# Moving the on-chip buffers of a matmul-bound attention + softplus-MLP kernel to other addresses

## The chip, the cores and the metric

The kernel runs on one core of a Trainium2 chip. The core has a matrix engine (TensorE, "PE" in the profile; its weight loads are listed apart as "PEld"), a vector engine (VectorE, DVE), a scalar engine (ScalarE, ACT), GpSimd (POOL), the SyncE queue that issues nearly all transfers here (SP), 16 DMA engines, a state buffer of 128 partitions (SBUF) and a matmul accumulator (PSUM). The metric is device microseconds of one execution; lower is better.

## The reference

Attention without a softmax, normalised per row, followed by an MLP with a softplus:

```
kv  = einsum('bhsd,bhse->bhde', k, v)          # B=8, H=8, S=576, D=64
o   = einsum('bhsd,bhde->bhse', q, kv)
x   = o / sqrt(mean(o*o, -1) + 1e-6) * g_norm  # then (B,H,S,D) -> (4608, 512)
h   = x @ w_in                                 # 512 -> 2048
g   = max(h, 0) + log1p(exp(-|h|))             # softplus
out = g @ w_out                                # 2048 -> 512
```

q, k and v come as float32, the weights as float64, of which the kernel reads the two 32-bit words.

## The kernel before, in words

Both factors of the large products are split into two or three float32r pieces, so that TensorE's products of pieces add up to the wanted precision. A buffer of pieces is therefore three times as long as its matrix. Every product on TensorE takes two operands from SBUF: the weights (`lhsT`, 128 x 128, loaded by a LDWEIGHTS) and the streamed operand (`rhs`, 256, 384 or 512 columns of 4 bytes in each partition). The weights of product i+1 are loaded while product i streams; in the trace such a load starts 2 to 5 ns after the start of product i in the dense stretches.

The work has two stages. In the first (`step`, L830; 64 steps up to about 360 us) blocks of 384 tokens go through weight chunks held in SBUF. `mm1` (L844) streams `units` with the weights `pieces`: twelve products of 384 columns. Softplus and the split of its result into `gv` follow on ACT and DVE, and `mm2` (L851) streams `pieces` (w_out) with the weights `gv`: three times three products of 512 columns. In between lie the attention (L677, L701, L719, L757), the conversion of the weights, and in the first 60 us warm-up products of the identity matrix (L1210) where TensorE would be idle.

In the second stage (`wide_step`, L1024; 48 steps, two passes over 9 groups of 512 tokens) the first product is formed from seven sub-products of half blocks: `product` (L1039, L1046) streams 256 columns of `units`, `early` or `turned` with weights from `pieces`, `w12` to `w14` or `half0` to `half2`. `mm2` (L1111, L1116) streams `pieces` (or a `w`) with weights from `gv0`/`gv1` (`gvt`) and `g0`/`g1` (`gt`). In both stages DVE and ACT make the pieces (L855, L859, L1095, L1103, L1106, L1109 for the results; L1006, L1009, L1012 for the inputs).

The order of all instructions on all engines is laid down by a planner (`Plan.order`, L90) from due times and assumed durations, before anything runs. It knows rings of slots and no addresses. Buffers come from two pools, `const` and `sb`. `space` (L286) makes a named buffer the first time it is asked for, and `new` (L314) hands it, or a part of it, to a slot; what `new` doesn't find by name it takes from `sb` under the slot's own tag, among them the small `r_0` and `r_1` of the row norms (`rows`, L688; L705 to L713). The allocator places buffers one after the other in the order in which they are first asked for, so that order decides the addresses.

The built program puts them, in bytes within a partition, here (the last number is the address modulo 512):

```
units    17312  416     raw      160672 416     half0  198560 416
pieces   54176  416     g1       164768 416     half1  201632 416
loads   127904  416     m_0..m_7 168864 416 ..  w14    204736 448
gv1     136096  416     w12      184224 416     half2  210912 480
early   144288  416     w13      192416 416     gv0    213984 480
g0      156576  416     ident_r   16512 128     turned 222176 480
```

All parts of buffers that TensorE takes begin at multiples of 512 bytes within them. So a streamed operand and the weights loaded meanwhile lie 0 bytes apart modulo 512 in 3,475 of the 4,581 float32r products, 32 or 64 bytes apart in 1,082, and otherwise in the rest (mostly beside `ident_r`). Apart from `ident_r` and `w14`, the operands begin at 32 modulo 64.

Of the kernel before, what the change touches and what calls it, by code (L numbers as in the profile page):

```python
# [8 lines left out]
F32 = mybir.dt.float32  # L9
F32R = mybir.dt.float32r  # L10
# [8 lines left out]
P = 128  # L19
# [7 lines left out]
def shaped(x, shape, dtype):  # L27

    n = 1
    for d in shape[1:]:  # L30
        n *= d
    words = n // 2 if dtype == BF16 else n
    x = x[:, :words]
    if x.dtype != dtype:
        x = x.bitcast(dtype)
    names = "abcdef"[:len(shape) - 1]
    if len(names) < 2:
        return x
    return x.rearrange(f"r ({' '.join(names)}) -> r {' '.join(names)}", **dict(zip(names, shape[1:])))
# [162 lines left out]
def kernel(  # L202
# [25 lines left out]
    B, H, S, D = q.shape  # L228
# [13 lines left out]
    WIDE = 512  # L242
# [25 lines left out]
    const = ctx.enter_context(tc.tile_pool(name="const", bufs=1))  # L268
    sb = ctx.enter_context(tc.tile_pool(name="sb", bufs=1))
# [8 lines left out]
    half = const.tile([P, H], F32, name="half")  # L278
    big = const.tile([P, 1], F32, name="big")
    over = const.tile([P, 2 * KF], F32, name="over")  # L280
    scale = const.tile([P, 1], F32, name="scale")

    PIECE = 3 * d_model
    spaces = {}

    def space(name, words, late, dtype=F32):  # L286

        if (name, late) not in spaces:
            spaces[name, late] = sb.tile([P, words], dtype, tag=name, name=f"{name}_{int(late)}")
        return spaces[name, late]  # L290

    units = sb.tile([P, 6, PIECE], F32R, name="units")
    pieces = sb.tile([P, 12, PIECE], F32R, name="pieces")
    loads = sb.tile([P, 4 * d_model], F32, name="loads")

    minus_r = space("gv1", 4 * WIDE, False, F32R)[:, 3 * NT:3 * NT + P]
    early = space("early", 2 * PIECE, False)
    kvs = [shaped(early[:, 2 * PIECE - (i + 1) * NP * D:2 * PIECE - i * NP * D], [P, NP, D], F32) for i in range(2)]
    tails = [shaped(space("g0", 2 * WIDE, False)[:, i * H * D:], [P, H, D], F32) for i in range(2)]
# [14 lines left out]
    def new(s, shape, dtype=F32):  # L314
        r, i = s.ring, s.place
        bank = {"h": i, "s0": 4, "s1": 5, "s2": 6, "tp": 7, "s3": 7}.get(r)
        if r == "o":
            s.tile = banks[:, 2:4].rearrange("r b (a k t) -> r (b a) k t", k=2, t=P)[:, :, i]
        elif r == "ab":
            s.tile = banks[:, 2 * i:2 * i + 2]  # L320
        elif bank is not None:
            s.tile = shaped(banks[:, bank], shape, dtype)
        elif r == "xv":
            s.tile = shaped(units[:, 3 * i:3 * i + 3].rearrange("r a b -> r (a b)"), shape, dtype)
        elif r == "qa":
            s.tile = shaped(early, shape, dtype)
        elif r in ("xb", "u1"):
            s.tile = shaped(space("turned", PIECE, r == "u1", F32R if r == "u1" else F32), shape, dtype)
        elif r == "u":
            s.tile = shaped(units[:, 2 * i:2 * i + 2].rearrange("r a b -> r (a b)") if i < 3 else  # L330
                            space("early", 2 * PIECE, True, F32R), shape, dtype)
        elif r == "w":
            s.tile = shaped(pieces[:, i] if i < 12 else space(f"w{i}", PIECE, True, F32R), shape, dtype)
        elif r == "n":
            s.tile = shaped(space(f"w{12 + i // 3}", PIECE, False)[:, i % 3 * d_model:], shape, dtype)
        elif r == "wh":
            s.tile = shaped(space(f"half{i}", PIECE // 2, True, F32R), shape, dtype)
        elif r == "gvp":
            s.tile = shaped(space(f"gv{i}", 4 * WIDE, True, F32R), shape, dtype)
        elif r == "gv":  # L340
            s.tile = shaped(space(f"gv{i}", 4 * WIDE, False, F32R), shape, dtype)
        elif r == "g":
            s.tile = shaped(space("half2", PIECE // 2, False)[:, i * NT:], shape, dtype)
        elif r == "x":
            s.tile = shaped(space(f"half{i}", PIECE // 2, False), shape, dtype)
        elif r == "rawb":
            s.tile = shaped(space("g1", 2 * WIDE, False), shape, dtype)
        elif r in ("e", "xl"):
            s.tile = shaped(loads[:, i * (d_model if r == "e" else 2 * d_model):], shape, dtype)
        else:  # L350
            s.tile = sb.tile(shape, dtype, tag=f"{r}_{i}", name=f"{r}_{i}")
        return s.tile
# [42 lines left out]
    def weight(j, pos, fetch_pos, behind):  # L395
# [5 lines left out]
        def fetch():  # L401
            src = w_source(j)
            x = new(raw, [P, d_model, words], U32 if wide else F32)
            nc.sync.dma_start(
                out=x.rearrange("p n w -> p (n w)").rearrange("p (a f) -> p a f", a=src.shape[1]), in_=src)

        f = add("SP", 450, fetch, (), fetch_pos, [raw], size=1800, behind=behind)
        if wide:
# [5 lines left out]
            def square():  # L414
                nc.scalar.activation(new(sq, [P, d_model], BF16), raw.tile.bitcast(BF16)[:, :, 3],
                                     func=AF.Square, scale=2.0 ** 47)

            def high1():
                nc.vector.tensor_scalar(out=new(t, [P, d_model], U32), in0=words_of()[1], scalar1=3,
                                        scalar2=0x3FFFFFF8, op0=ALU.logical_shift_left, op1=ALU.bitwise_and)  # L420
# [825 lines left out]
```

## Time and profile before

| | |
|---|---|
| median of 3 runs | 875.08 us (872.5 to 876.75) |
| the profiled execution: span from first to last instruction | 869.7 us |
| TensorE busy, share of the span | 853.5 us, 98% |
| VectorE busy | 704.4 us, 81% |
| ScalarE busy | 521.9 us, 60% |
| moved by DMA | 167 MB, 192 GB/s |

The profiled execution is known by its span alone; it ends 5.4 us below the median and 2.8 us below the fastest run, which is what lies before its first and after its last instruction, and the spread of the runs.

TensorE's products overlap in the profile: the "mean ns of one" is a product's time from its start to its modelled end, while the next one starts earlier. What a product costs is the distance from its start to the start of the next one, called its pitch here. The chain of work shows it: so many products in so many microseconds.

### The profile page before, as it was taken

The page shows a single profiled execution, that of the slowest core. Times are in us where ns is not written, and L with a number is a line of the kernel's source. Part 1 is how long each engine was busy: PE and PEld are TensorE (multiplying, and loading weights), DVE is VectorE, ACT ScalarE, POOL GpSimd, SP SyncE. Part 2 cuts the span into 40 slices and gives each one's busy share as a digit, 9 for nine tenths or more (in the row PEclk, how much of TensorE's full clock was granted, in tenths as well). Part 3 has the DMA queues.
Part 4 walks back from the last instruction along what each step waited for, and adds up shares of the span by engine and source line. Part 5 has one row for each costly group of instructions (what it writes and reads, how often), then busy time and mean ns, then how long its engine had stood idle before and what let it go on. Part 6 is the DMA issues. An engine that isn't in the chain of part 4 may idle for free.

```text
span 869.7 us, 17041 instructions
## 1 busy us (share of the span) xinstructions
PE 853.5 (98%) x6464; PEld 758.2 (87%) x6464; DVE 704.4 (81%) x995; ACT 521.9 (60%) x980; POOL 75.9 (9%) x79
## 2 busy tenths in 40 slices
PE   7799999999999999999999999999999999999998
PEld 5578888888888999988999988898999899999996
DVE  7888889888788888898888798878788766788873
ACT  5766665436344467766667655654867555566654
POOL 0351223111113300000000000000000000000000
PEclk9999999999999999999999999999999999999999
DMA  9999998989894755436655546545364752777864
GB/s 267 281 243 209 265 239 262 178 243 216 216 183 120 186 168 176 146 99 216 202 155 163 171 148 205 189 150 170 121 196 139 230 165 96 237 239 240 242 188 127
DMA packets 239778, 167.07 MB, mean 192 GB/s; under 512 B 106320, under 2 KB 198736, under 8 KB 239696
## 3 DMA queue, kind: packets, MB, share of 16 engines
q1 hardware_dynamic: 239392, 165.86, 68.4%
q8 instruction: 50, 0.82, 0.4%
q14 instruction: 32, 0.26, 0.1%
q10 hardware_dynamic: 304, 0.13, 0.1%
HBM read 112.98 MB, written 52.95 MB: 191 GB/s over the span
## 4 chain that ended last, share of the span: by engine, by line
PE 94%; DMA 3%; DVE 2%; ACT 1%; issue 0%; POOL 0%; SPq 0%; DVEq 0%; ACTq 0%
PE banks L1116 31%; PE banks L1046 28%; PE banks L851 16%; PE banks L844 15%; PE banks L701 2%; PE banks L677 2%; DMA early<-in_q_dram 1%; DMA loads<-in_v_dram 1%; DMA g<-in_v_dram 1%; DMA raw<-in_moe_w_in_dram 0%; PE banks L719 0%; PE banks L1210 0%; DVE units L624 0%; DVE half L713 0%; DVE units L627 0%
## 5 line engine op out<-in xcount | busy, mean ns | idle before, releaser
L1116 PE MATMUL banks<-pieces,gv 128*128 128x512 f32 x768 | 240.2, 394 | 0.0
L1116 PE MATMUL banks<-pieces,g_False 128*128 128x512 f32 x384 | 150.2, 391 | 0.0
L1116 PEld LDWEIGHTS banks<-pieces,gv 128*128 128x128 f32 x768 | 133.1, 189 | 19.1
L851 PE MATMUL banks<-pieces,gv 128*128 128x512 f32 x576 | 145.8, 397 | 0.0
L844 PE MATMUL banks<-units,pieces 128*128 128x384 f32 x768 | 145.3, 337 | 0.0
L844 PEld LDWEIGHTS banks<-units,pieces 128*128 128x128 f32 x768 | 135.3, 188 | 5.0
L851 PEld LDWEIGHTS banks<-pieces,gv 128*128 128x128 f32 x576 | 106.1, 188 | 21.1
L1046 PEld LDWEIGHTS banks<-units,pieces 128*128 128x128 f32 x840 | 112.7, 190 | 7.0 <-ACT banks L1091 0.4
L1046 PE MATMUL banks<-units,pieces 128*128 128x256 f32 x840 | 116.9, 282 | 0.0
L866 ACT ACTIVATE half<-banks 128x384 f32<-128x384 f32 x64 | 31.4, 491 | 95.2 <-PE banks L844 93.9
L1106 DVE TENSOR_TENSOR gv<-g_True,gv 128x1024 fp32r<-128x1024 f32 x47 | 57.5, 1223 | 37.4 <-ACT gv L1103 37.4
L1116 PEld LDWEIGHTS banks<-pieces,g_False 128*128 128x128 f32 x384 | 72.1, 188 | 16.1
L1046 PEld LDWEIGHTS banks<-units,w 128*128 128x128 f32 x504 | 67.6, 189 | 4.1 <-ACT banks L1091 0.2
L1046 PE MATMUL banks<-units,w 128*128 128x256 f32 x504 | 70.5, 282 | 0.0
L709 POOL TENSOR_TENSOR r<-r,half 128x8 f32<-128x8 f32 x36 | 62.3, 1730 | 3.0
L1109 DVE SCALAR_TENSOR_TENSOR g_False<-gv 128x1024 fp32r<-128x1024 f32 x47 | 57.6, 1225 | 1.5
L1095 DVE TENSOR_TENSOR g_True<-banks,g_True 128x512 f32<-128x512 f32 x48 | 33.1, 690 | 30.7 <-PE banks L1046 24.6
L1009 DVE TENSOR_TENSOR units<-loads,units 128x1024 fp32r<-128x1024 f32 x42 | 51.2, 1219 | 6.4 <-ACT units L1006 6.3
L1073 ACT ACTIVATE g_True<-banks 128x256 f32<-128x256 f32 x96 | 36.8, 384 | 32.6 <-PE banks L1046 31.9
L911 ACT ACTIVATE m<-banks 128x512 f32<-128x512 f32 x72 | 42.1, 595 | 19.7 <-PE banks L1116 13.8
L1012 DVE SCALAR_TENSOR_TENSOR units<-units 128x1024 fp32r<-128x1024 f32 x42 | 51.4, 1224 | 1.8
L1006 ACT ACTIVATE units<-loads 128x1024 fp32r<-128x1024 f32 x42 | 44.4, 1058 | 12.5 <-PE banks L1046 12.5
(115 smaller groups left out, 1248.1 us busy)
## 6 DMA issues: line engine op xcount, KB each, us to landing
loads<-x SPq DMA_DIRECT2D x180, 128.0 KB, 2.6
part<-m SPq DMA_DIRECT2D x72, 256.0 KB, 3.0
m<-part SPq DMA_DIRECT2D x72, 256.0 KB, 3.4
loads<-form SPq DMA_DIRECT2D x45, 256.0 KB, 3.3
form<-loads SPq DMA_DIRECT2D x36, 256.0 KB, 2.9
raw<-in_moe_w_in_dram SPq DMA_DIRECT2D x16, 512.0 KB, 4.6
loads<-in_k_dram SPq DMA_DIRECT2D x32, 256.0 KB, 4.6
loads<-in_v_dram SPq DMA_DIRECT2D x32, 256.0 KB, 4.6
```

What stands on the lines that cost most here:

```text
L709: nc.gpsimd.tensor_tensor(out=r.tile, in0=r.tile, in1=half, op=ALU.pow)
L844: nc.tensor.matmul(hp, lhsT=w_in.tile[:, i, kd * P:(kd + 1) * P], rhs=xv.tile[:, i, kd], start=(m == 0), stop=(m == 3 * KD - 1))
L851: nc.tensor.matmul(mine[i].tile, lhsT=gv.tile[:, m, i * P:(i + 1) * P], rhs=w_out.tile[:, m], start=(c == cs[0] and m == 0), stop=(c == cs ...
L911: a = add("ACT", 690 if ph == LAST else 600, lambda: nc.scalar.activation(new(ot, [P, d_model]), bank.tile, func=AF.Copy, scale=scale if p ...
L1006: nc.scalar.activation(part_of(0, F32R), xl.tile if m > 1 else xl.tile[:, 0], func=AF.Copy, scale=DOWN)
L1009: nc.vector.tensor_tensor(out=part_of(1, F32R), in0=xl.tile if m > 1 else xl.tile[:, 0], in1=part_of(0), op=ALU.subtract)
L1012: nc.vector.scalar_tensor_tensor(out=part_of(2, F32R), in0=part_of(1), scalar=-RADIX, in1=part_of(0), op0=ALU.mult, op1=ALU.add)
L1046: nc.tensor.matmul(place(q), lhsT=w[:, m, at:at + P], rhs=dst.tile[:, m, v, kd] if u < 6 else dst.tile[:, m, kd], start=(u == 0 and not m ...
L1073: nc.scalar.activation(dst, src, func=AF.Softplus, scale=1.0 + E)
L1106: nc.vector.tensor_tensor(out=gvt(1, F32R), in0=gt(), in1=gvt(0), op=ALU.subtract)
L1109: nc.vector.scalar_tensor_tensor(out=gt(F32R), in0=gvt(1), scalar=-RADIX, in1=gvt(0), op0=ALU.mult, op1=ALU.add)
L1116: nc.tensor.matmul(mine[i].tile, lhsT=(gvt(m, F32R) if m < 2 else gt(F32R))[:, c, i * P:(i + 1) * P], rhs=outs[c].tile[:, m], start=fresh ...
```

## The change

Only addresses change. A small constant tile `roots` takes the place of the two `r` buffers, and `gap0` fills up to a multiple of 64 bytes. All buffers with streamed `units`, `early`, `turned` and all weights of `mm2` (`gv`, `g`) are asked for first and begin at 0 modulo 512; 256 bytes of `gap1` follow, and then the buffers of weight pieces, whose addresses are 256 modulo 512, and everything that is only for ACT, DVE and DMA.

```diff
+    roots = const.tile([P, 2, H], F32, name="roots")
+    const.tile([P, 8], F32, name="gap0")
 
     PIECE = 3 * d_model
+    SHIFT = 64
...
     units = sb.tile([P, 6, PIECE], F32R, name="units")
+    for i in (0, 1):
+        space(f"gv{i}", 4 * WIDE, False, F32R)
+        space(f"g{i}", 2 * WIDE, False)
+    space("early", 2 * PIECE, False)
+    space("turned", PIECE, False)
+    sb.tile([P, SHIFT], F32, name="gap1")
     pieces = sb.tile([P, 12, PIECE], F32R, name="pieces")
+    for i in range(3):
+        space(f"w{12 + i}", PIECE, False)
+        space(f"half{i}", PIECE // 2, False)
     loads = sb.tile([P, 4 * d_model], F32, name="loads")
...
+        elif r == "r":
+            s.tile = roots[:, i]
```

The instructions of every engine, their order and their waits are the same in the two built programs, one by one; only the addresses and names of buffers differ. Afterwards the distance modulo 512 is 256 in 4,078 of the 4,581 float32r products, 0 in 479 (where `mm1` or `product` hands over to `mm2` or back, and among the warm-ups) and 128 in the rest, and every operand begins at a multiple of 64.

## The prediction

> **What bounds the kernel now.** I read the page's shares first, then the chain that ended last, then the stages, then single stretches of TensorE.
>
> ```profile
> span 869.7 us, 17041 instructions
> PE 853.5 (98%) x6464; PEld 758.2 (87%) x6464; DVE 704.4 (81%) x995; ACT 521.9 (60%) x980; POOL 75.9 (9%) x79
> PEclk9999999999999999999999999999999999999999
> PE 94%; DMA 3%; DVE 2%; ACT 1%; issue 0%; POOL 0%; SPq 0%; DVEq 0%; ACTq 0%
> ```
>
> TensorE is the bound: 94% of the chain is its own products, at full granted clock, so waits are a small matter. What counts is the pitch, the time from one product's start to the next one's. The chain in order of time gives it, as stretches of one line:
>
> ```profile
> 0.72 3.74 DMA raw<-in_moe_w_in_dram
> 6.61 5.81 DMA g<-in_v_dram
> 12.90 6.89 DMA early<-in_q_dram
> 19.81 6.71 DMA loads<-in_v_dram
> ...
> 129.71 4.18 PE banks L851 x18
> 138.36 4.17 PE banks L844 x24
> ...
> 444.24 2.85 PE banks L1046 x24
> 454.76 2.86 PE banks L1046 x24
> 457.63 2.78 PE banks L1116 x12
> ```
>
> Per product: 256 columns 2.86/24 = 119.2 ns (L1046), 384 columns 4.17/24 = 173.8 ns (L844), 512 columns 4.18/18 = 232.2 ns (L851) and 2.78/12 = 231.7 ns (L1116). What would be the pitch without a loss? In the first 3 us, before TensorE speeds up, warm-up products of 512 columns start 426 to 427 ns apart in the trace; at exactly double that rate they would be 213.3 ns apart, 0.4167 ns a column, so 106.7, 160.0 and 213.3 ns for the three widths. Against this each product now loses 12.5, 13.8, 18.9 and 18.4 ns. Products by line: 2016 (L1046), 768 (L844), 576 (L851), 1152 (L1116). Together 25.2 + 10.6 + 10.9 + 21.2 = 67.9 us. That is the most there is to win on TensorE.
>
> Next, what stands behind TensorE in the stages (columns: PE, PEld, DVE, ACT, POOL busy):
>
> ```profile
> 60.00:130.00 70.00, 69.44 (x714) 60.35 (x713) 61.39 (x106) 42.67 (x85) 16.94 (x17) 1.00 0.99 241
> 130.00:360.00 230.00, 230.00 (x1943) 205.70 (x1942) 194.15 (x334) 122.02 (x241) 41.23 (x40) 1.00 0.76 188
> 360.00:460.00 100.00, 100.00 (x635) 90.58 (x634) 88.49 (x112) 67.15 (x127) 0.00 (x0) 1.00 0.55 174
> 660.00:760.00 100.00, 100.00 (x624) 89.88 (x623) 71.96 (x78) 57.99 (x104) 0.00 (x0) 1.00 0.55 176
> ```
>
> From 70 us on TensorE never stands still; DVE is next, 88% busy at worst.
>
> **Does the distance of the addresses matter at all?** Three readings, from the start times in the trace joined with the allocator's addresses. First, the pitch of equal products at equal distances isn't constant: at distance 0 the 256-column pitch runs from 112 to 134 ns, and whole sequences (116, 119, 119, 121, 116, 118) come back to the nanosecond in different steps, whatever DMA and the other engines do. A fixed cost of issue would be one number; so TensorE's stream and its own weight load disturb each other, depending on how they stand to each other. Second, small distances change it a little, with both signs:
>
> ```profile
> 505.19 1.59 PE L1046 MATMUL banks<-units,pieces 128*128 128x256 f32 x12
> 506.62 0.63 PE L1116 MATMUL banks<-pieces,gv 128*128 128x512 f32 x2
> ...
> 508.03 0.87 PE L1046 MATMUL banks<-turned,half 128*128 128x256 f32 x6
> 508.74 1.59 PE L1046 MATMUL banks<-units,w 128*128 128x256 f32 x12
> ```
>
> From start to start, `units` with `pieces` (0 apart) takes 1.43 us for twelve, 119.2 ns each; `turned` with `half1` (64 apart) 0.71 us for six, 118.3. Over the whole trace distances of 32 and 64 have 117.0 to 118.3 against 119.1 to 119.9 at 0. For 512 columns it is the reverse: triples of L1116 with `gv0` (two of three weight loads 64 off) have a mean pitch of 231.7 ns, with `gv1` (all at 0) 229.5. Third, the few products nearest to the new distance, 224 or 288 bytes, beside `ident_r`: 512 columns at 228, 228, 236 and 229 to 234 ns, 384 columns at 174, which is no gain. In all of them one of the two operands begins at 32 modulo 64. Both at multiples of 64 and 256 apart isn't in this trace; both at multiples of 64 and 0 apart is (warm-ups), at 226 to 240 ns.
>
> **The change part by part.** (1) Pitch of TensorE. 4,078 of 4,581 float32r products get the new distance, nine in ten of each line. Ends: all of the loss goes, 67.9 x 0.9 = 61 us; below nothing, if every one takes the worst spacing that is common now (236 ns, 178 ns, 122 ns: 1728 x 4.1 + 768 x 4.2 + 2016 x 2.8 = 16 us, x 0.9), 14 us are lost. I take a value between: each product at the best spacing that the trace has for its width under disturbance, 225, 170 and 113 ns. That is 1728 x 6.9 + 768 x 3.8 + 2016 x 6.2 = 11.9 + 2.9 + 12.5 = 27.3 us, x 0.9 = 25 us. I choose it because the first reading shows that the relation of the two streams sets the pitch and the third forbids counting on the whole.
>
> (2) What is late next. With 25 us gone, 100 us of the second stage become 97, beside DVE's 88.5 at worst; the handovers ACT to DVE to TensorE, now hidden, show at some places, mostly in 360 to 460 us. I give back a tenth, 3 us (from nothing to a quarter, 6).
>
> (3) DMA. All transfers from and to SBUF begin elsewhere (multiples of 64 and of 256). The chain has four transfer waits, 3.74 + 5.81 + 6.89 + 6.71 = 23.2 us, all before 27 us. Fetches of 128 KB land after 4.6, 4.9, 5.5 and 5.9 us (page, part 6) at various places, 12% around their middle: 0, from -2.8 to +2.8 us. Later transfers lie under TensorE.
>
> (4) DVE, ACT, POOL. The same instruction has the same duration at either offset: L1106 into `gv0` (480) and `gv1` (416) is 1215 to 1228 ns throughout. `roots` is 32 bytes a row, as `r` was. 0, and they lie under TensorE.
>
> Sum: 25 - 3 = 22 us off. The profiled span is 869.7 us and the median 5.4 above it; I subtract from the median: 875.1 - 22 = 853 us.
>
> [...]
>
> **The rivals.** *The loss goes wholly* (no disturbance once the two reads are half of 512 bytes apart). For it: the loss is nearly one constant per product, 12 to 19 ns over a doubling of the width, as the weight load is. Against it: the products at 224 and 288. Price: 61 us, and DVE at 88.5 of then 93 us gives back about a sixth: 51 off, 824 us.
>
> *Nothing happens*: the disturbance doesn't come from addresses (a shared path to SBUF, say), and distance only shifts a rhythm whose mean stays. For it: the third reading, and the warm-ups on aligned addresses at about 231. Price: parts (3) and the small differences, 0 +- 4 us: 875.
>
> *Slower*: the new distance locks products into the long spacing. The mechanism is the one row that goes that way, L1116 with `gv0`, 2.2 ns longer than with `gv1`. All at 236, 178 and 122 ns, 14 us: 889 us. It decides from a mean of 1 ns more per product on (4,078 x 1.0 ns = 4 us).
>
> **How the numbers follow.** Chances: the part case 0.40, all of it 0.20, nothing 0.17, slower 0.23. A measurement of this kernel can tell about 0.5%, 4.4 us, from no change. Faster by more than that: both first cases, 0.60; within: 0.17; slower: 0.23. The likeliest gives 853, with its own range of 843 to 868 (gain 10 to 35 us, give-back 0 to 6). The range for 8 in 10 goes down to 820 (all of it with 6 us to spare) and up to 886; what it leaves out is the slower half of the slower case, 0.12, and a rest of the first.
>
> **What would show it.** The chain after: x24 of L1046 in 2.70 to 2.75 us, x24 of L844 near 4.10, x18 of L851 near 4.06, x12 of L1116 near 2.70 would be the part case; 2.64, 3.93, 3.90 and 2.60 or less all of it; 2.86, 4.17, 4.18, 2.78 nothing. Pitches that no longer wander within one line would show that the disturbance is gone; new waits of TensorE for DVE in 360 to 460 us that the give-back is real; the four first transfer waits answer part (3). The prediction is wrong if the pitch moves by under 1 ns on average or upwards, or if an engine behind TensorE takes most of the gain.

## The result, and the profile after

The changed kernel takes 869.26 us (median of 7 runs, 868.5 to 871.7) beside 873.27 us (7 runs, 872.5 to 876.75) of the kernel before: ratio 0.9954, 95% interval 0.9937 to 0.997. That is 4 us, 0.46%, less than the 0.5% that the prediction set as its bound for a change that a measurement can tell, though the interval leaves 1 out. Forecast were 22 us. The granted clock of TensorE explains little of it: in the runs whose mean granted clock is 1.000, the spans average 870.5 us before (8 runs) and 867.1 us after (3 runs).

The page of the changed kernel, TensorE's share and the main transfer queue:

```profile
span 867.5 us, 17041 instructions
PE 853.9 (98%) x6464; PEld 760.3 (88%) x6464; DVE 704.4 (81%) x995; ACT 521.3 (60%) x980; POOL 76.6 (9%) x79
...
q1 hardware_dynamic: 239392, 165.86, 64.5%
```

The same queue in the kernel before (packets, MB, share of the time of 16 DMA engines):

```profile
q1 hardware_dynamic: 239392, 165.86, 68.4%
```

TensorE is as busy as it was (853.9 us beside 853.5). The transfers, the same in number and bytes, take less of the DMA engines' time (64.5% beside 68.4%). The chain of the changed kernel in order of time (start, length, what; lines are 14 later than before):

```profile
124.27 4.18 PE banks L858 x24
128.45 4.12 PE banks L865 x18
...
452.95 2.87 PE banks L1060 x24
455.82 2.75 PE banks L1130 x12
```

Per product 174.2, 228.9, 119.6 and 229.2 ns, where the kernel before had 173.8, 232.2, 119.2 and 231.7. So products of 512 columns became a little shorter, those of 256 and 384 a little longer. Over the whole trace, with the distance from start to start of every product that has no gap behind it (called mean pitch from here on): 256 columns 118.89 to 119.27 ns, 384 columns 174.97 to 175.16, 512 columns 231.38 to 230.26. On 2,016, 768 and 1,728 products that is +0.77, +0.15 and -1.94 us, 1.0 us less in all.

The rest lies at the beginning. The first `mm1` products of the chain in the changed kernel:

```profile
44.61 2.11 PE banks L858 x12
...
64.49 2.10 PE banks L858 x12
```

and in the kernel before:

```profile
45.77 2.11 PE banks L844 x12
...
65.68 2.11 PE banks L844 x12
```

They start 1.2 us earlier, and this lead stays. Which transfers became quicker over the whole run is seen in the issues (engine, count, KB each, median us from issue to landing), though all but three of these come after the first 45 us. Before:

```profile
early<-in_q_dram SPq DMA_DIRECT2D x48, 144.0 KB, 5.1
x<-turned SPq DMA_DIRECT2D x28, 192.0 KB, 4.8
```

After:

```profile
early<-in_q_dram SPq DMA_DIRECT2D x48, 144.0 KB, 3.9
x<-turned SPq DMA_DIRECT2D x28, 192.0 KB, 3.6
```

Both are cut into small packets. By their sizes the fetches into `early`, with 12 smaller stores out of `turned`, are the 61,440 packets of 128 bytes, and the 28 stores out of `turned` the 14,336 of 384 bytes. Packets of 128 bytes took 16.9 ns on average before (13 in the middle, 29 at the 90th of 100) and 12.8 after (13 at both places), those of 384 bytes 28.2 and 24.6.

So there were two theories to test. *Transfers*: the gain comes for the most part from where transfers begin, and TensorE's loss of 12 to 19 ns a product has little to do with addresses. *Distance*: the 256 bytes between stream and weights give the gain, and the loss is a disturbance of the two reads that was only partly removed.

### The profile page after: what moved, and what is told of

The parts are those of the page before. It is cut to its first block, busy times and chain, and to the rows that moved or that the text cites. A ratio compares the mean times of both kernels' runs of the same rounds, so it can differ in the third digit from the quotient of the medians.

```text
span 867.5 us, 17041 instructions
## 1 busy us (share of the span) xinstructions
PE 853.9 (98%) x6464; PEld 760.3 (88%) x6464; DVE 704.4 (81%) x995; ACT 521.3 (60%) x980; POOL 76.6 (9%) x79
## 3 DMA queue, kind: packets, MB, share of 16 engines
q1 hardware_dynamic: 239392, 165.86, 64.5%
## 4 chain that ended last, share of the span: by engine, by line
PE 94%; DVE 1%; ACT 1%; POOL 0%; issue 0%; ACTq 0%; DVEq 0%
PE banks L1130 31%; PE banks L1060 28%; PE banks L865 16%; PE banks L858 15%; PE banks L715 2%; PE banks L691 2%; PE banks L733 0%; DVE units L638 0%; DVE half L727 0%; PE banks L1224 0%; POOL roots L723 0%; DVE units L641 0%; DVE roots L719 0%; DVE m L459 0%; ACT units L635 0%
## 5 line engine op out<-in xcount | busy, mean ns | idle before, releaser
L723 POOL TENSOR_TENSOR roots<-roots,half 128x8 f32<-128x8 f32 x36 | 62.3, 1731 | 3.0
L869 DVE TENSOR_TENSOR gv<-half,gv 128x384 fp32r<-128x384 f32 x64 | 35.4, 553 | 20.6 <-ACT gv L882 19.9
```

The source lines that it names most:

```text
L723: nc.gpsimd.tensor_tensor(out=r.tile, in0=r.tile, in1=half, op=ALU.pow)
L869: nc.vector.tensor_tensor(out=gv.tile[:, 1], in0=g.tile, in1=gv.tile.bitcast(F32)[:, 0], op=ALU.subtract)
```

## The experiments

### Series of products in isolation

`pitch` runs nothing but series of 24 products of TensorE, each series on its own source line, with warm-ups ahead. Two of the lines, L52 and L59, broken here to fit:

```python
for i in range(N): nc.tensor.matmul(banks[:128, 1, :512], lhsT=buf[:, 2048 + 128 * (i % 4):2048 + 128 * (i % 4) + 128],
        rhs=buf[:, 0 + 512 * (i % 2):0 + 512 * (i % 2) + 512], start=(i == 0), stop=(i == N - 1), skip_group_check=True)  # d0
for i in range(N): nc.tensor.matmul(banks[:128, 1, :512], lhsT=buf[:, 2112 + 128 * (i % 4):2112 + 128 * (i % 4) + 128],
        rhs=buf[:, 0 + 512 * (i % 2):0 + 512 * (i % 2) + 512], start=(i == 0), stop=(i == N - 1), skip_group_check=True)  # d256
```

> Leaves the whole computation out: 35 series of 24 products of TensorE each, one after the other, each series with one relation of the two operands (its output is zeros). Theory T (the chip's two reads disturb each other by something that isn't the address, and the rhythm's mean is what it is): all distances 0 to 448 with 512 columns have a mean pitch of 228 to 233 ns, and 256, 384 and 512 columns keep 119, 174 and 231 at distance 0 and 256; the operand's place modulo 64 changes nothing over 1 ns. Rival B (banks by address): at least one distance of aligned operands is under 222 ns. If the loss comes from 4-byte operands, the bfloat16 series are at 214 to 218 ns; if it comes from the weight load, series with 64 and 32 weight columns fall by a half and three quarters of the 12 to 18 ns; if from either alone, the other series stay at 231.

Its chain (start, length, what). L52, L55, L57, L59: 512 columns of 4 bytes, weights 0, 64, 128 and 256 bytes away modulo 512. L67, L68: 256 columns at 0 and 256. L69: 384 at 0. L75: 512 columns with 32 weight columns in place of 128. L80: the streamed operand is one element, read 512 times. L82, L84: 512 and 256 columns of 2-byte operands (bfloat16).

```profile
28.36 5.44 PE banks L52 x24
...
44.84 5.60 PE banks L55 x24
...
56.05 5.60 PE banks L57 x24
...
67.15 5.45 PE banks L59 x24
...
111.36 2.87 PE banks L67 x24
114.23 2.88 PE banks L68 x24
117.11 4.17 PE banks L69 x24
...
141.78 5.56 PE banks L75 x24
...
169.12 5.25 PE banks L80 x24
...
179.83 5.20 PE banks L82 x24
...
190.20 2.62 PE banks L84 x24
```

Divided by 24, or over the last 16 distances between starts of each series, to 0.1 ns:

| series, 512 columns unless told | pitch, ns |
|---|---|
| distance 0, 16, 256 | 226.7 |
| 192, 448 | 228.7 |
| 384 | 232.3 |
| 32, 64, 128, 320 | 233.3 |
| 96 | 234.3 |
| both operands at 32 modulo 64: distance 0, 256 | 226.9, 226.7 |
| both at 16, at 4 modulo 64, distance 0 | 231.2, 233.3 |
| weights 80 KB away, distance 0, 256 | 226.7, 226.7 |
| the same weights each time; another PSUM bank each time | 226.7; 226.7 |
| 64, 32 weight columns | 229.7, 231.6 |
| streamed operand one element | 218.6 |
| 2-byte operands: distance 0, 256 | 215.9, 215.9 |
| 256 columns: 4-byte at 0, 256; 2-byte | 119.6, 120.0; 109.1 |
| 128 columns: 4-byte at 0, 256 | 111.7, 111.7 |

This answers most of it. Distances do differ: 226.7 to 234.3 ns, where 228 to 233 had been expected. But a distance of 256 is the same as a distance of 0 (226.7 ns both), and both are among the best there is for 512 columns; nothing could be gained by moving from the one to the other. Multiples of 64 bring TensorE nothing over 32 (226.7 and 226.9), while places at 16 and 4 cost 4 to 7 ns, against what was expected. The loss is counted against the prediction's estimate of 0.4167 ns a column, 2.4 columns a ns; the 2-byte series have that slope, 0.417 ns a column from 109.1 ns at 256 columns to 215.9 at 512. A smaller weight load doesn't shorten the loss: 64 and 32 weight columns have 229.7 and 231.6 ns, the same weights each time 226.7. 2-byte operands have 2.5 ns in place of 13.3 (512 and 256 columns alike), and a stream that reads one element over and over has 5.3. So in these series it comes with streaming 4-byte operands from changing addresses. Below 256 columns the pitch stops falling with the width: 128 columns have 111.7 ns, as 64 and 192 have in `pitch2` below.

### One half of the change at a time

`align_only` is the changed kernel without the distance:

```diff
-    SHIFT = 64
...
-    sb.tile([P, SHIFT], F32, name="gap1")
```

> The change without the 256 bytes between the groups: every operand and weight at 0 modulo 512, all buffers at multiples of 64. Theory T with a second part (the opening gains about 1.2 us because transfers begin at multiples of 64): time as the changed kernel, 867 to 870 us, opening 1.2 us shorter than before, the pitch within 0.5 ns of the changed kernel. Rival B (the distance of 256 gives the gain): time as before, 872 to 875, x12 of the 512-column products back at 2.78 us.

Measured 869.3 us (6 runs), ratio to the kernel before 0.9946 (0.9929 to 0.9963). Mean pitches 119.27, 175.11 and 230.25 ns, and in the chain the first `mm1` where the changed kernel has it:

```profile
44.61 2.09 PE banks L856 x12
```

`shift_only` is the changed kernel without the fill to 64 bytes, so that all buffers begin at 32 modulo 64:

```diff
-    const.tile([P, 8], F32, name="gap0")
```

> The change without the fill to 64 bytes: operands and weights 256 apart modulo 512, everything at 32 modulo 64. Theory T: the opening as before (its 1.2 us lost), time 871 to 875 us. Rival B (the distance gives the gain): 867 to 870 us, and the 512-column x12 at 2.75 us.

Measured 872.83 us (12 runs), ratio 0.9991 (0.9978 to 1.0005). Its pitches are those of the changed kernel too, 119.26, 175.09 and 230.29 ns, but the opening is late and packets of 128 bytes are back at 17.5 ns:

```profile
46.76 2.08 PE banks L857 x12
```

The distance theory has fallen: the 256 bytes do nothing (119.27, 175.16 and 230.26 ns with them, 119.27, 175.11 and 230.25 without). The 1 us of pitch is there with or without the fill; what is gained in the opening goes with where the buffers begin (`mm1` at 44.61 us with the fill, at 46.76 without).

### Which buffers, and which multiples

`transfers_off` shifts by 32 bytes those buffers alone that TensorE doesn't read in these products:

```diff
+    sb.tile([P, 8], F32, name="gap2")
     loads = sb.tile([P, 4 * d_model], F32, name="loads")
```

> The changed kernel with 32 bytes before the buffers that only transfers, ACT and DVE use (loads, raw, m), which then begin at 288 modulo 512; TensorE's operands stay where the change puts them. If the opening's gain comes from where transfers begin: 0.6 to 1.2 us of the opening come back, pitch as in the changed kernel, 868.5 to 871 us. If it comes from TensorE's operands or by chance: as the changed kernel, 867 to 870 us.

Measured 869.81 us (9 runs, up to 872.33), ratio 0.9959 (0.9946 to 0.9973). The pitches stay (119.28, 175.16, 230.30), packets of 128 bytes keep their 13.0 ns, and yet the opening is late again:

```profile
46.44 2.09 PE banks L859 x12
```

The profile gives back the whole of the opening, the median half a microsecond of it; the profiled run (871.14) is one of the slower ones.

`operands_off` is the counterpart, without `gap0` and with `gap2`: operands at 32 modulo 64, `loads`, `raw` and `m` at multiples of 256.

> TensorE's operands all at 32 modulo 64 and 256 apart, the buffers loads, raw and m at multiples of 256: the counterpart of the run that shifted loads, raw and m alone. Packets of 128 bytes go into early (q) and out of turned, which are off here, and have their long tail again (over 25 ns at the 90th of 100). If these slow packets cost the opening: 871 to 873.5 us. If loads, raw and m carry it: 869 to 870.5. Pitch of TensorE as in the changed kernel.

Measured 870.55 us (12 runs, 869.05 to 874.67), ratio 0.9976 (0.9961 to 0.9992): between the two kernels. `mm1` at 45.17 us, packets of 128 bytes at 16.4 ns with their tail (28 at the 90th). By these openings (46.44 and 45.17 us beside 44.61) both groups have a share; neither run says how much to better than half.

`align192` begins everything at 192 modulo 256, a multiple of 64 (`SHIFT` and `gap1` are left out as in `align_only`):

```diff
-    const.tile([P, 8], F32, name="gap0")
+    const.tile([P, 56], F32, name="gap0")
```

> As the aligned kernel without the 256 bytes, but everything begins at 192 modulo 256 and at a multiple of 64. If multiples of 64 are what transfers need: 868 to 870.5 us, packets of 128 bytes at 13 ns up to the 95th of 100, as in the changed kernel. [...] Pitch as in the aligned kernel either way.

Measured 871.87 us (12 runs), ratio 0.9981 (0.9971 to 0.9991). Pitches 119.27, 175.12, 230.26; `mm1` at 46.18 us; packets of 128 bytes at 16.7 ns, as before the change. So beginning at a multiple of 64 doesn't make these packets quick. Put together by the place modulo 256 of the two buffers with 128-byte packets, `early` and `turned`:

| kernel | place modulo 256 | 128-byte packets: mean, middle, 90th of 100, ns |
|---|---|---|
| changed, `align_only`, `transfers_off`, `apart128`, `apart64` | 0 | 12.8 to 13.2, 13, 13 |
| before | 160 (`early`), 224 (`turned`) | 16.9, 13, 29 |
| `align192` | 192 | 16.7, 13, 28 |
| `shift_only`, `operands_off` | 224 | 17.5 and 16.4, 13, 31 and 28 |

At 0 no packet of 128 bytes that begins at a multiple of 128 crosses a multiple of 256; at 160, 192 and 224 every second one does, and a part of the packets is slow: 22 of 100 took over 20 ns before, 0.4 of 100 after. That the slow ones are the ones that cross is not shown. Packets of 2 KB have no such difference: 84 ns in the middle before, after and in `align192`.

The opening goes with the place of all transferred buffers, in a grouping made after the results. In the four profiles of kernels whose transferred buffers all begin at multiples of 128 (two of the changed kernel, `align_only`, `apart128` below) the first `mm1` starts in the chain at 44.2 to 44.9 us, in the seven profiles of kernels with some of them elsewhere at 45.2 to 47.1.

The packets of 128 bytes are not the way there. In none of the eleven profiles does one start before 40.4 us, in the two of the kernel before not before 42.8 us, and by then the products are already late: compared product by product, these two lie 1.9 and 2.1 us behind the changed kernel at 26 us, and 1.2 and 2.3 us at 41 us. `transfers_off`, and `apart64` below, have these packets at 13 ns and a late opening. Up to 40 us transfers go mostly in packets of 256 bytes and more; those of 256 take 22.1 and 23.4 ns on average before and 18.3 and 18.7 after, but `transfers_off` has 18.7 too. Through which transfer the place of the buffers would delay the opening stays open.

### Distances again

`apart128` has 128 bytes in place of 256, which the isolated series gives 233.3 ns at 512 columns:

```diff
-    SHIFT = 64
+    SHIFT = 32
```

> The change with 128 bytes between the groups in place of 256. In the isolated series 512 columns at distance 128 had 233.3 ns against 226.7 at 0 and at 256. If that carries over: the 512-column pitch rises from 230.3 to 232 to 234 ns, 3 to 6 us on 1,728 products, 872 to 876 us with the opening as in the changed kernel. If the kernel's own changes of rhythm wash it out: 869 to 870.5 us.

Measured 873.87 us (11 runs), ratio 1.0008 (0.9999 to 1.0017). The opening is the best of all (`mm1` at 44.23 us), and yet it is 4.6 us behind the changed kernel, for the mean pitch of 512 columns is 232.29 ns (+2.0, 3.5 us), of 384 columns 175.93 (+0.8, 0.6 us), of 256 columns 119.09 (-0.2, 0.4 us). In its chain:

```profile
128.35 4.18 PE banks L865 x18
...
446.87 2.78 PE banks L1130 x12
```

The pitches add up to 3.7 of the 4.6 us. So the distance does count, by 2 ns of 230, and it counts modulo 256: in `pitch`, 0 and 256, 64 and 320, 192 and 448 have the same pitch (226.7, 233.3 and 228.7 ns), 128 and 384 differ by 1.0. `pitch2` and `pitch3` are more series, of other widths and of distances in steps of 16.

> Leaves the whole computation out: 26 more series of 24 products (output zeros). In the first series 4-byte operands of 128, 256, 384 and 512 columns lost 13 ns each against 2.4 columns a ns, 2-byte ones 2.5. If the loss belongs to the streamed operand's start, it is one number for all widths from 256 to 512 (320 columns at 146.7, 448 at 200 ns), it stays at 13 ns with weights that are one repeated column, and in the series that alternates 2-byte and 4-byte products only the 4-byte products are long (216 and 227). If it belongs to the loading of 4-byte weights, the products beside which such weights are loaded are long, which there are the 2-byte ones, and repeated-column weights shorten it. Distances of 32 to 224 bytes with 256 and 384 columns change the pitch by under 3 ns, as with 512 they made 226.7 to 234.

In the chain of `pitch2`, 320 and 448 columns (L55, L57), 512 columns with one weight column repeated (L61), 256 columns at distance 64 (L68):

```profile
35.51 3.52 PE banks L55 x24
...
43.20 4.96 PE banks L57 x24
...
58.89 5.49 PE banks L61 x24
...
95.27 2.73 PE banks L68 x24
```

320 columns have 146.7 ns, again 13.3 above the estimate of 2.4 columns a ns (128 columns, named with the others in the expectation, lie 58 above it with their 111.7); 448 have 206.7, 20 above, not the 200 that was expected. Counted in the time of 16 columns (6.67 ns, 64 bytes in a partition), 256, 320, 384, 448 and 512 columns take 18, 22, 26, 31 and 34 for 16, 20, 24, 28 and 32 of their own. Repeated weights don't shorten the product (228.6). At 256 columns the distance of 64 takes 113.3 ns, 17 such units in place of 18: there distances change the pitch by up to 6.7 ns, more than expected. The series that alternates 2-byte and 4-byte products says nothing: a pair takes 460 ns, more than 216 and 227, with recorded starts 422 and 38 ns apart.

> Leaves the whole computation out: 48 series of 24 products, 256, 384 and 512 columns, weights 0 to 240 bytes (steps of 16) beyond the streamed operand modulo 256 (output zeros). Known so far: 256 columns have 120.0 ns at 0 and 113.3 at 64; 384 have 173.3 at 0 and 174.9 at 64; 512 have 226.7 at 0 and 233.3 at 64. If pitch goes by place modulo 256 alone, these come back to 0.1 ns. Theory T as it now stands (a constant of the 4-byte stream of about two times 16 columns, and a rhythm of some ns on top that depends on the distance): no distance brings 512 columns under 222 or 256 under 112. Rival B: some distance between the steps tried so far does.

Of 16 distances, 256 columns are best at 64 and else at 116.6 to 120.4; 384 columns lie at 173.3 to 177.3; 512 columns at 226.7 for 0, 16 and 240 and up to 234.3 elsewhere. L52 and L56 are 256 columns at 0 and 64, L84 and L88 512 columns at 0 and 64:

```profile
26.99 2.87 PE banks L52 x24
...
38.37 2.72 PE banks L56 x24
...
139.42 5.48 PE banks L84 x24
...
161.53 5.59 PE banks L88 x24
```

No distance brings 512 columns under 222 ns or 256 under 112: against the estimate of 2.4 columns a ns 13.3 ns stay at 512 columns, 13.3 at 384 and 6.7 at 256. For 256 columns there is little left to gain, for 64, 128 and 192 columns all have 111.7 ns. That this floor is the loading of 4-byte weights would fit the length of a weight load (188 ns for 128 weight columns, 134 for 64, 109 for 32 in `pitch`, 0.84 ns a column); it is not shown, for no series with short products and fewer weight columns was run. But distance alone doesn't fix the pitch. 384 columns at 64 have 173.4 ns here and 174.9 in `pitch2`, 256 columns at 96 and 128 have 117.4 and 120.2 here, 120.0 and 118.4 there: the same series can settle in two rhythms.

### A version that beats both

The two widths of the second stage want different distances: 64 where `product` streams 256 columns (113.3 ns in the series, beside 120.0 at 0), 0 where `mm2` streams 512 (226.7 beside 233.3 at 64). `apart64` gives both, by moving the weights of `mm2` to the side of the weight pieces:

```diff
-    SHIFT = 64
+    SHIFT = 16
...
-    for i in (0, 1):
-        space(f"gv{i}", 4 * WIDE, False, F32R)
-        space(f"g{i}", 2 * WIDE, False)
     space("early", 2 * PIECE, False)
...
         space(f"half{i}", PIECE // 2, False)
+    for i in (0, 1):
+        space(f"gv{i}", 4 * WIDE, False, F32R)
+        space(f"g{i}", 2 * WIDE, False)
+    sb.tile([P, 64 - SHIFT], F32, name="gap2")
```

> The changed kernel with other places modulo 256: units, early and turned at 0, the weight pieces and the weights gv and g of the second product at 64, loads, raw and m at 0. Distance 64 for 256 and 384 columns, 0 for 512. If the isolated series carry over: the 256-column pitch falls from 119.3 by 3 to 6 ns (6 to 12 us on 2,016 products), 384 columns rise by 1 to 1.6 ns (1 us), 512 stay at 230; 859 to 865 us, faster than both kernels. If short sequences never reach the good rhythm: 867 to 871 us.

Measured 862.67 us (6 runs, 861.25 to 865.19), ratio to the kernel before 0.9876 (0.9858 to 0.9894). From its chain:

```profile
139.43 4.19 PE banks L859 x24
...
453.32 2.83 PE banks L1061 x24
456.15 2.72 PE banks L1131 x12
```

Mean pitches 117.74 ns at 256 columns (-1.5 against the changed kernel, 3.1 us), 175.88 at 384 (+0.7, 0.6 us) and 227.36 at 512 (-2.9, 5.0 us). The gain at 256 is a quarter of what the series has. The larger one, at 512, was not expected: the distance there is 0 modulo 256 in both kernels.

The trace shows where both come from, when the pitch is averaged by place within a sequence (second stage, from one product to the next of its width). At 512 columns the changed kernel's first five places have 233.3, 235.8, 228.5, 232.4 and 230.9 ns, and from the sixth on 226.6 to 226.8, the settled pitch of the series; most of its sequences are 3, 6, 9 or 12 products long. `apart64` has 226.6 to 226.9 from the first place on. So it is spared an unsettled start, a run-in, that costs the changed kernel 3.7 of the 5.0 us. The isolated series show such a run-in too: in the last one of `pitch`, at distance 0 and behind 2-byte products, a spacing of 312 ns and nine of 225 to 236 come before the steady 226 and 227. At 256 columns the products of `apart64` are steady from the first place on as well, at 117.3 to 118.3 ns by place, but not at the series' 113.3: they settle in another rhythm. What decides which rhythm a sequence falls into, and why the products with weights 64 bytes away hand over to `mm2` without a run-in, no run isolates.

The opening of `apart64` is late (`mm1` at 47.12 us), with `gv`, `g` and `w12` to `w14` at 64 modulo 256; a version with these at a multiple of 128 as well was not run.

### How much the opening scatters

> The kernel before, a second profile, for the spread of its opening. If the changed kernel's gain of 1.2 us up to 76 us comes from transfers and not from chance, this one passes the product that began at 74.96 us in the changed kernel at 75.8 us or later; the pitches come back to 0.05 ns (118.89, 174.97, 231.38). If the opening scatters by more than a microsecond, it lies anywhere from 74.5 to 77.5.

> The changed kernel, a second profile. From transfers: the same product at 74.5 to 75.4 us; pitches 119.27, 175.16, 230.26 again. From chance: 74.5 to 77.5.

The kernel before passes the product named there at 77.23 us (76.15 in the first profile), the changed kernel at 75.22 (74.96). At 133 us, where TensorE no longer waits (it is busy for all of 133 to 860 us in the first profile of each kernel), it is 132.86 and 134.63 beside 131.54 and 131.82: 2.1 us less on average, with 1.8 us of scatter in the kernel before and 0.3 in the changed one. From there to the last product both pairs agree to 0.04 us: 730.77 and 730.73 before, 729.95 and 729.97 after. So pitch gives 0.8 us from there on, surely; the opening about 2 us, of which two profiles each tell no more than the size; the sum, 2.9, is 1.1 short of the difference of the medians, which is less than the scatter of one opening.

## Why the prediction was wrong

It has the direction, and the time lies in the range, but 22 us were forecast and 4 came.

**The step that failed is (1), the pitch:** "each product at the best spacing that the trace has for its width under disturbance", 25 us. Measured are 0.8 to 1.0 us. Over all 4,512 products that is 0.2 ns each, under the 1 ns that the prediction named as its sign of being wrong. Two things were wrong in it.

The loss against the estimate of 2.4 columns a ns was taken for a disturbance between stream and weight load because the pitch wanders (112 to 134 ns at 256 columns). The series show two parts: one that no distance, no other weights and no smaller weight load removes (13.3 ns at 384 and 512 columns, 6.7 at 256, but 2.5 with 2-byte operands), and a wandering of some ns on top of it. Only the second depends on distance. A steady pitch is not a short one, either: in the changed kernel's second stage the 256-column pitch is 119.9 to 120.0 ns from the seventh place of a sequence on, where it was 118.4 to 120.0 before. It has nearly stopped wandering, and it is longer.

And 256 was taken for a new distance. It is the old one: what counts is the distance modulo 256 (226.7 ns at 0 and at 256), and 3,475 of 4,581 products were at 0 before. The spacings hoped for (225, 170 and 113 ns) were not far from what the series reach at their best distances (226.7, 173.3 and 113.3); the step that failed is that 256 bytes would take the products there.

What the change did move are the 1,082 products at 32 and 64. The prediction's second reading had these right in sign and nearly in size. Product by product, the 482 of 256 columns among them went from 118.1 to 119.4 ns (+0.65 us), the 572 of 512 columns from 231.9 to 230.2 (-1.00 us). Another 0.95 us came from the 1,150 products of 512 columns whose distance modulo 256 stayed 0; that a neighbour's rhythm carries over to them would fit, but is not shown.

The third reading, products beside `ident_r` at 224 and 288 bytes without any gain, spoke plainly for "nothing happens" and was put aside, because one operand in each was at 32 modulo 64. The series show that this place costs TensorE nothing (226.9 against 226.7), so the reason had no row behind it. But the rows themselves were not near: at 512 columns distances of 32 and 224 have 233.3 ns where 0 and 256 have 226.7, so products at 224 and 288 could not tell what happens at 256, in either direction. If they seemed to foretell the result, it was by luck.

**(2), the give-back,** had no object: with 1 us gained on TensorE, nothing behind it came late.

**(3), the transfers,** was taken at 0 between -2.8 and +2.8 us. About 2 us less was measured in the opening, within these ends; that is a larger share of the 4 us than the pitch has. Its sign, the four first transfer waits, can't be read one for one: the changed kernel's chain can be followed back only to 34 us. What was missing is the place of the transferred buffers modulo 128, which goes with the opening in all eleven profiles (first `mm1` at 44.2 to 44.9 us with all at multiples of 128, else at 45.2 to 47.1); by which transfer stays open.

**(4), the other engines,** was right: VectorE is busy for 704.4 us in both kernels, ScalarE for 521.9 and 521.3.

**The rivals.** "Nothing happens", at 0.17, comes nearest, in what it said of the pitch too: "distance only shifts a rhythm whose mean stays", within 2 ns (between 256 and 128 bytes the mean pitches differ by 0.2, 0.8 and 2.0 ns). Distance is not worth nothing, though: 128 bytes in place of 256 cost 4.6 us, and the kernel with 64 bytes beside the 256- and 384-column streams gained 6.6. "The loss goes wholly" is excluded by the series (226.7 ns at best at 512 columns, where it would need 213.3). What "slower" named was measured at another distance: with 128 bytes the pitch of 512 columns rises by its 2 ns, from 230.26 to 232.29.

## What to carry to other kernels

That a pitch wanders, as it did here from 112 to 134 ns at one width and one distance, does not show how much of it can be removed; a short program with series of one instruction, one line each, tells the constant from the wandering part for the price of one run. Rows are near only where the effect is smooth: here 32 bytes took the pitch from 226.7 to 233.3 ns, so the nearest rows could neither support nor refute the change, and a reason for leaving rows aside must itself be seen in a row. Transfers deserve a look of their own when buffers move: packets of 128 bytes took 16.9 ns at one place and 12.8 at another. But what they cost must be looked for at the time when something waits for them; here the quicker packets came mostly after the opening.

## What the runs showed that was not expected

- At distance 0 the settled pitches of 4-byte products of 256 columns and more come in whole units of 16 columns (6.67 ns): 18, 22, 26, 31 and 34 for 256, 320, 384, 448 and 512 columns, and 17 for 256 columns with the weights 64 bytes on. What makes the two or three units stays open; that they go with streaming 4-byte operands from changing addresses is shown, by the series with 2-byte operands (215.9 ns at 512 columns) and with one element (218.6).
- Mean pitches come back to 0.1 ns in every kernel here with the same distances modulo 256 (119.26 to 119.28, 175.09 to 175.19, 230.25 to 230.31 in seven profiles), wherever the buffers lie and whatever the transfers do.
- A stream that goes over the same 64 bytes again and again is slower than one through fresh addresses: 242.0 ns against 226.7 at 512 columns; over 256 bytes it is 226.6 (`pitch2`).
